# A transformer block moved to even/odd token pairs in the two row halves of TensorE, with DMA transposes, 121-query blocks, two-bank PSUM groups and a mixed phase order

## The chip, the cores and the metric

The kernel runs on one core of one Trainium2 chip. The metric is device time in microseconds (us) of one execution; "span" is the same thing inside one profiled execution, a few us shorter. TensorE is called PE, its weight loads PEld, VectorE DVE, ScalarE ACT, GpSimd POOL, and SP is the engine that issues the DMAs. PSUM is the memory that matmuls write; results are copied out of it by ACT or DVE. The granted clock is the share of its full clock that PE got. This is a one-core program, and a run counts as slow when it is more than 1.5% above the fastest of its kernel.

## The reference, cut to what matters

Two blocks in series on 2048 tokens of width 448, all bf16. The attention has 16 heads of 28, and each query sees 8 keys two tokens apart. So even tokens only attend to even ones and odd tokens to odd ones.

```python
h  = x + A(layernorm(x), wqkv, wo)            # attention: keys at t, t-2, ..., t-14
h2 = h + B(layernorm(h), w1, w2, w3, w4)
# B(y): g = gelu(layernorm(y) @ w1); shift g's four channel groups by -1, +1, -2, +2 tokens
#       x1 = y + shifted(g) @ w2;  x1 + gelu(layernorm(x1) @ w3) @ w4      (w3: 448 x 1792)
```

So a token passes three layernorms, and each is followed by a transpose (tokens to columns) and a projection.

## The kernel before

The kernel is written as a list of operations in *program order*. A planner on the host then fixes an order for each engine: it always takes the operation that can start earliest, and among those within 100 ns of each other the one written first. It knows durations from constants in the code. On the chip every engine works through its fixed order; semaphores hold it where data is missing. So the order in which phases are written matters in two ways: it breaks ties, and it decides who gets a shared buffer first, because a later-written user of a buffer waits for the earlier-written one.

The contraction of 448 is cut in four pieces of 112 rows. Layernorm output is transposed on PE, through PSUM, and copied out by ACT or DVE:

```python
    def transposes(ls, dst):
        for half in range(2):
            T = tile()
            for il in range(4):
                for cc in range(2):
                    c = 2 * half + cc
                    S.add("pe", "transpose", 64.0,
                          out=T(lambda p, o=cc * 512 + il * 128: p[0:KC, 0, :].bitcast(BF16)[:, o:o + 128]),
                          in_=lntm[:, ls, il, c * KC:(c + 1) * KC], identity=ident[:])
            copy(dst(half), T(...), 1024, 0.52)
    # QK: for each of 8 tiles: 4 matmuls, 112 rows, 128 weights columns, 512 tokens
    # W3: for each of 14 tiles: 4 matmuls, 112 rows, 512 tokens; gelu by ACT, 512 wide
```

The phases are written unmixed (cut):

```python
    phase_A1(0) ... phase_QK(0); phase_V(0); ... phase_att(0); phase_QK(1) ... phase_att(3)
    phase_WO(2); phase_WO(3)
    phase_B1(0); phase_B1(1); phase_B2(0); phase_B1(2); phase_B1(3)      # layernorm 2, W1; W2
    phase_W3(0); phase_B2(1); phase_W3(1); phase_B3(0); ...              # layernorm 3, W3; W4
```

## Time and profile before

252.07 us median of 3 runs. First the page of the profiled execution: busy time per engine, then PE's busy share and granted clock in 40 equal slices (a digit is tenths), then the engines' shares of the chain that ended last (work and waits followed back from the last instruction), then three groups of instructions (count, busy us, mean ns of one). All have one line number, L1100 here, because one line of the kernel issues every operation.

```profile
span 250.6 us, 4082 instructions
...
PE 224.6 (90%) x1681; PEld 112.9 (45%) x1681; DVE 138.2 (55%) x306; ACT 120.7 (48%) x175; POOL 46.2 (18%) x71
...
PE   0799799999979998898995999899998999899992
...
PEclk9999659999965995589998899999999999999998
...
PE 72%; DVE 16%; ACT 5%; POOL 2%; issue 2%; DVEq 0%
...
L1100 PE MATMUL ps<-actT,w_s 112*128 112x512 bf16 (+1 forms) x288 | 64.2, 382 | 1.2 <-DVE mv L1100 1.1
...
L1100 PE MATMUL ps<-ident,lntm 128*112 128x128 bf16 x192 | 18.8, 250 | 11.2 <-DVE lntm L1100 11.2
...
L1100 ACT ACTIVATE pt<-ps 110x1024 bf16<-110x1024 f32 x32 | 30.3, 1030 | 7.8 <-PE ps L1100 7.8
```

PE is the bound: it is busy 90% of the span and it is 72% of the chain. The clock row shows 5 and 6 in three places in the first half. They follow stretches like this one, from the timeline of PE (start us, duration, what, and what ended the idle time before it):

```profile
66.82 1.24 PE L1100 MATMUL ps<-qT,kT 28*110 28x103 bf16 x40
68.39 0.46 PE L1100 MATMUL ps<-qT,kT 28*110 28x103 bf16 x10 [0.33 <-ACT pt L1100]
69.30 0.46 PE L1100 MATMUL ps<-qT,kT 28*110 28x103 bf16 x10 [0.46 <-ACT pt L1100]
70.22 0.46 PE L1100 MATMUL ps<-qT,kT 28*110 28x103 bf16 x10 [0.46 <-ACT pt L1100]
```

PE works 0.46 us and waits 0.46 us, because each pair of heads needs one exponential of 1 us on ACT (the ACT line above).

For the comparison I break a span into terms. *Work*: every matmul at its full-clock pace in the traces (216 ns for 512 columns, 189 for 448, 56 for 128; where two or four matmuls run side by side, that divided by two or four). *Switches*: 96 ns for each change between full, half-row, quarter-row and quarter-column tiles, read from the gaps in the trace. *Half clock*: the work of the matmuls that started before the first clock record or in a half-clock record, counted once more. *First* and *tail*: before PE's first and after its last matmul. *Waits*: the rest. Work and half clock are estimates from these durations; the other terms are read directly.

| | span | work | switches | half clock | first | tail | waits |
|---|---|---|---|---|---|---|---|
| before | 250.6 | 193.1 | 5.5 | 18.1 | 7.0 | 4.8 | 22.2 |

### The profile page before, as it was taken

To read this page: it belongs to the slowest core of one execution; us is meant where nothing else is said; L and a number is where in the kernel's file an instruction comes from. 1 tells how busy PE (TensorE), PEld (TensorE's weight loads), DVE (VectorE), ACT (ScalarE), POOL (GpSimd) and SP (SyncE) were. 2 spreads that over 40 slices of the span, in tenths; PEclk is the share of its full clock that TensorE was granted. 3 is DMA by queue.
4 is the path that set the end of the run, shared out by engine and by line. 5 is a ranking of instruction groups with operands and counts; after the bars stand their busy time and mean duration, and the time that the engine had idled before them with its cause. 6 is when DMAs were issued, how large, how long until landed. Compare 5 with 4: busy or idle time off the path is not lost.

```text
span 250.6 us, 4082 instructions
## 1 busy us (share of the span) xinstructions
PE 224.6 (90%) x1681; PEld 112.9 (45%) x1681; DVE 138.2 (55%) x306; ACT 120.7 (48%) x175; POOL 46.2 (18%) x71
## 2 busy tenths in 40 slices
PE   0799799999979998898995999899998999899992
PEld 0336345645533556354544533533554345533550
DVE  7596862595785677877999602700385008700220
ACT  2468836896485649645422575166002740156000
POOL 8512200010031003003017200800016000710000
PEclk9999659999965995589998899999999999999998
DMA  6999900070610052007000000000100000000111
GB/s 164 291 222 232 275 12 5 8 171 5 146 29 0 8 131 44 3 7 173 0 1 3 0 0 0 21 18 0 36 15 25 0 16 23 20 18 0 42 39 42
DMA packets 11696, 14.07 MB, mean 56 GB/s; under 512 B 2136, under 2 KB 10712, under 8 KB 11160
## 3 DMA queue, kind: packets, MB, share of 16 engines
q1 hardware_dynamic: 11672, 13.75, 22.7%
q8 instruction: 15, 0.25, 0.4%
q14 instruction: 9, 0.07, 0.1%
HBM read 11.65 MB, written 1.97 MB: 54 GB/s over the span
## 4 chain that ended last, share of the span: by engine, by line
PE 72%; DVE 16%; ACT 5%; POOL 2%; issue 2%; DVEq 0%
PE ps L1100 72%; DVE st L1100 4%; DVE lntm L1100 4%; ACT pt L1100 3%; DVE xb L1100 2%; POOL rstd L1100 2%; DVE mv L1100 1%; DVE oT L1100 1%; ACT hT L1100 1%; ACT actT L1100 1%; DVE pt L1100 1%; ACT arena L1100 0%; POOL vtmp L1100 0%; DVE xin L1100 0%; DVE msk L1100 0%
## 5 line engine op out<-in xcount | busy, mean ns | idle before, releaser
L1100 PE MATMUL ps<-actT,w_s 112*128 112x512 bf16 (+1 forms) x288 | 64.2, 382 | 1.2 <-DVE mv L1100 1.1
L1100 ACT ACTIVATE arena<-ps 128x512 bf16<-128x512 f32 (+1 forms) x67 | 40.0, 597 | 28.0 <-PE ps L1100 27.8
L1100 PE MATMUL ps<-w_s,arena 128*128 128x448 bf16 x224 | 43.9, 353 | 0.0
L1100 PEld LDWEIGHTS ps<-actT,w_s 112*128 112x128 bf16 (+1 forms) x288 | 25.9, 106 | 37.8 <-ACT arena L1100 15.2
L1100 PE MATMUL ps<-hT,arena 112*128 112x512 bf16 x128 | 39.4, 453 | 0.5 <-ACT hT L1100 0.2
L1100 DVE TENSOR_TENSOR ost<-ps,xb 128x448 bf16<-128x448 f32 x16 | 10.0, 622 | 54.2 <-PE ps L1100 54.1
L1100 ACT ACTIVATE pt<-ps 110x1024 bf16<-110x1024 f32 x32 | 30.3, 1030 | 7.8 <-PE ps L1100 7.8
L1100 ACT ACTIVATE actT<-ps 112x1024 bf16<-112x1024 bf16 x10 | 10.0, 1028 | 44.2 <-PE ps L1100 44.2
L1100 POOL TENSOR_SCALAR vtmp<-mv 128x4 f32<-128x4 f32 (+1 forms) x19 | 4.6, 241 | 143.0 <-DVE mv L1100 142.3
L1100 PEld LDWEIGHTS ps<-w_s,arena 128*128 128x128 bf16 x224 | 21.5, 98 | 20.5 <-DVE xb L1100 0.6
L1100 PE MATMUL ps<-ident,lntm 128*112 128x128 bf16 x192 | 18.8, 250 | 11.2 <-DVE lntm L1100 11.2
L1100 PEld LDWEIGHTS ps<-ident,lntm 128*112 128x112 bf16 x192 | 15.9, 152 | 14.5 <-DVE lntm L1100 12.1
L1100 DVE TENSOR_TENSOR pt<-pt,msk 110x1024 bf16<-110x1024 bf16 x32 | 21.0, 684 | 1.7 <-ACT pt L1100 1.7
L1100 DVE BATCH_NORM_STATS2 st<-xin 128x6 f32<-128x448 bf16 x32 | 19.2, 601 | 2.4 <-DMA xin<-in_A_x_dram 1.9
L1100 PEld LDWEIGHTS ps<-hT,arena 112*128 112x128 bf16 x128 | 11.6, 108 | 17.9 <-issue 6.0
L1100 POOL TENSOR_TENSOR rstd<-vtmp,mhalf 128x4 f32<-128x4 f32 (+1 forms) x19 | 18.5, 972 | 1.6
L1100 POOL TENSOR_TENSOR xb<-xb,xin 128x448 bf16<-128x448 bf16 x16 | 16.7, 1072 | 1.5 <-DVE lntm L1100 1.5
L1100 DVE TENSOR_TENSOR xb<-ps,xb 128x448 bf16<-128x448 f32 x16 | 9.6, 600 | 13.4 <-PE ps L1100 13.1
L1100 PE MATMUL ps<-qT,kT 28*110 28x103 bf16 (+1 forms) x320 | 13.2, 229 | 3.8 <-ACT pt L1100 3.5
L1100 PE MATMUL ps<-wo_s,oT 128*128 128x448 bf16 x64 | 16.2, 403 | 0.4 <-DVE oT L1100 0.3
L1100 PE MATMUL ps<-arena,hT 112*110 112x448 bf16 x80 | 15.8, 353 | 0.0
L1100 ACT ACTIVATE gT<-ps 112x512 bf16<-112x512 f32 x16 | 9.6, 600 | 12.3 <-PE ps L1100 12.3
(52 smaller groups left out, 188.5 us busy)
## 6 DMA issues: line engine op xcount, KB each, us to landing
rzb<-rz_scratch SPq DMA_DIRECT2D x16, 256.0 KB, 4.4
w_s<-in_B_w_dram SPq DMA_DIRECT2D x2, 1568.0 KB, 18.0
out_dram<-ost SPq DMA_DIRECT2D x16, 112.0 KB, 1.7
xin<-in_A_x_dram SPq DMA_DIRECT2D x3, 448.0 KB, 8.9
arena<-in_A_wqkv_dram SPq DMA_DIRECT2D x3, 392.0 KB, 6.2
w_s<-in_B_w_dram SPq DMA_DIRECT2D x2, 392.0 KB, 10.5
xin<-in_A_x_dram SPq DMA_DIRECT2D x4, 112.0 KB, 2.2
wo_s<-in_A_wo_dram SPq DMA_DIRECT2D x4, 98.0 KB
```

The costliest lines, as they stand in the source:

```text
L1100: inst = getattr(eng, op.meth)(**op.kw)
```

## The change

Even and odd tokens go to separate banks of PSUM and to separate halves of the PE rows. 448 = 7 x 64: seven pairs of 64-row matmuls, each pair side by side, replace four 112-row matmuls per token. Layernorm output is transposed by DMA, straight into the row-half layout. Attention uses 121 queries against 128 keys, so that the weights are 128 columns and four row groups run at once. Results leave PSUM two banks at a time. The planner learns macros, tile modes and two-bank groups. Cut to its core:

```diff
+    def ln_to_HT(slot, kind, m, src):              # m: one of 8 blocks of 128 token pairs
+        sl = lctr[0] % NL                          # NL = 3 buffers of one block each
+        lctr[0] += 1
+        for a in range(2):
+            normalize(slot, kind, 2 * m + a, ln[:, sl, :, a, :], src[:, 2 * m + a, :]...)
+        S.add("sp", "dma_start_transpose", 1400.0, chan=ch("tr"), lat=128 * 896 * 2,
+              out=HT[:, :, 16 + 128 * m:16 + 128 * m + 128], in_=ln[:, sl, ...])
...
+    def phase_QK(u):
+        for c in range(4):
+            T = tile(2)
+            for w in range(2):
+                for b in range(KB):                # 7 pieces of 64
+                    for a in range(2):             # even tokens: rows 0-63; odd: rows 64-127
+                        ... mm(T(p[:, a, 256 * w:...]), wqk_p[half[a], b, ...], HT[half[a], b, 256 tokens])
+            copy(QK[...], T(p.rearrange("p a (w n) -> p a w n", w=2)), 1024)
...
+    def wload(chan, dst, src):                     # half-row weights are loaded twice
+        for u in range(2):
+            dma(chan + "ab"[u], dst[half[u]], src.rearrange("(b k) n -> k b n", k=64), ...)
...
+    setup()                                        # x0, x1, Q/K and V weights, x2..x7
+    for m in range(4):
+        phase_LN1(m)
+    weights()                                      # WO, W1, W2, W3, W4: 5.9 MB
+    unit_qkv(0); phase_att(0); unit_qkv(1); phase_LN1(4); phase_LN1(5); phase_att(1)
+    wo_ln2(0, 1, 2)
+    unit_qkv(2); phase_W1(0, 1); phase_W1(1, 2)
+    phase_LN1(6); phase_LN1(7); phase_att(2)
+    for m in (0, 1): phase_W2(m); phase_LN3(m)
+    phase_W3(0); unit_qkv(3); phase_W4(0); wo_ln2(3, 4); phase_att(3); phase_W1(3, 2)
+    ...
```

The change also *mixes* the MLP phases among the attention phases.

## The prediction

> **What bounds it now.** TensorE. Busy per engine: PE 224.6 of 250.6 us (90%), DVE 138, ACT 121. The chain that ended last is 72% PE. Start-to-start times from the trace, full clock: 512-column matmuls 216 ns, 448-column 189 ns, transposes 56 ns, the 28-row score matmuls 25 ns each (two at once), the 32-column value matmuls 13 ns (four at once). Times the counts: Q/K 128 x 216 = 27.6, V 80 x 189 = 15.1, transposes 192 x 56 = 10.8, W1 13.8, W3 48.4, W4 42.3, W2 and WO 12.1 each, scores 8.0, values 4.2: 194 us. The other 56 us: 7 us until the first transpose (10.4 until the first projection), some 5 us of tail, and about 40 us of waits and half clock. The clock records show 37 us at half clock in four stretches, three starting just after PE was paced by the exponentials (1 us each) in an attention stage, the fourth after the wait for the layernorm near 131-134 us. I put their cost at 18 us.
>
> **What the change does to PE.** 448 = 4 x 112 = 7 x 64: two 64-row matmuls, even and odd tokens, run side by side, so 7 half passes cost 3.5 instead of 4. If a pair of N columns takes what one full matmul takes (N/2.4 + 2.5 ns), I estimate Q/K 24.9, V 11.9, W1 12.5, W3 43.5. W4, W2, WO stay. Scores: four row groups at once and 288 instead of 320 matmuls, about 3.9; values 3.9. Transposes leave PE (-10.8). Sum 167 us: 27 us less. The 128-key block also brings the fast weight load, which the Trainium skill ("TensorE: Matmul & The Clock Gate", Weight-path perf modes) ties to 128 weights; the trace agrees in kind: 98 ns for a 128-column load, 130 ns for 110.
> Added: tile-mode switches, 96 ns each in the trace (56 now). I count about 100 after: +4 us.
>
> **Other engines.** The transposes' PSUM copies go (about 21 us of ACT and DVE); PSUM evictions get wider and fewer. 24 DMA transposes appear; no trace has one; I guess 4 us each until landed, hidden by other phases except at the start. Weights for half rows load twice (about 3 MB more), the Q/K ones before the first matmul: at the 290 GB/s seen early, the first projection starts near 13.5 us instead of 10.4. SP issues more, still far from full.
>
> **Critical path.** PE is the bound, so nearly all of the 27 us counts; start +3, switches +4. MLP phases are mixed among attention phases, so PE has fill work while exp runs; I expect waits and half clock to fall from 40 us to 15-20 but not vanish: the first two attention stages still have little fill work. 167 + 10 (switches) + 13.5 (start) + 4.5 (tail) + 15-18 = 210-213.
>
> **Predicted:** 211 us, 8 in 10 between 198 and 227. Faster by over 2%: 0.95; within 2%: 0.03; slower: 0.02.
>
> **Right or wrong, by the profile:** pairs of 64-row matmuls starting a few ns apart, a pair of 256 columns every 110 ns or so; PE's sum of start-to-start work near 167 us plus switches; half-clock time in the slices under 20 us, sitting before 80 us; no ident transposes; DMA transposes landing in 3-5 us; first matmul of Q/K at 12-15 us.
>
> **What would make it wrong:** pairs not overlapping (weight loads in series or a PSUM conflict: +40 us); DMA transposes landing in 8 us or more, starving W1 and W3; attention still pacing PE so the clock halves as before (+10 to 20); DVE, now reading two banks at a time, becoming the pacer in the early stages; or much better mixing, with no half clock after 30 us (below 200).

## The result

283.81 us median of 4 runs against 251.68 before. The ratio of the fast runs is 1.128 (95% interval 1.122 to 1.134): slower by 13%. Ratios here are the mean time of one kernel's fast runs over that of the other's of the same rounds, so not quite the ratio of the medians quoted.

The page after, with the lines that answer to those before:

```profile
span 280.3 us, 5851 instructions
...
PE 192.5 (69%) x2567; PEld 128.4 (46%) x2567; DVE 138.4 (49%) x296; ACT 102.0 (36%) x109; POOL 51.3 (18%) x92
...
PE   0009640699906540999999935569996489999892
...
PEclk9999955599986796699999977599999669999999
...
PE 59%; DMA 17%; DVE 11%; ACT 6%; issue 3%; POOL 2%; SPq 1%; DVEq 0%
...
L1259 PE MATMUL ps<-HT,w_s 64*128 64x256 bf16 (+1 forms) x1064 | 61.7, 279 | 19.2 <-DMA HT<-ln 10.8
```

And one line of the view of the DMAs (count, median us from issue to landing):

```profile
HT<-ln SPq DMA_TRANSPOSE x24, 2.9
```

PE is busy 32 us *less* and the span is 30 us *longer*. The half-row group shows that the core of the idea works: 1064 matmuls in 61.7 us are 58 ns each although one lasts 279, so pairs overlap. No identity transposes are left. But PE's row has zeros and fours in it, and DMA, which was not in the chain before, is 17% of it. The last line gives the transposes' median time to landing, 2.9 us, which is no worse than predicted.

| | span | work | switches | half clock | first | tail | waits |
|---|---|---|---|---|---|---|---|
| before | 250.6 | 193.1 | 5.5 | 18.1 | 7.0 | 4.8 | 22.2 |
| after | 280.3 | 165.2 | 5.9 | 19.4 | 21.6 | 4.9 | 63.3 |

The 28 us of work are gained, as predicted. 15 are lost at the start and 41 in waits. Who waits, from the waits view (us in total, times, longest):

```profile
PE ps L1259 <- DMA HT<-ln: 42.2, 3, 21.6
...
PE ps L1259 <- DVE pt L1259: 13.7, 6, 7.1
...
PE ps L1259 <- DVE QK L1259: 7.8, 2, 5.9
...
PE ps L1259 <- DVE xb L1259: 4.9, 1, 4.9
```

Three waits for a transposed layernorm make 42 us. One is the start, 21.6 us. The second is this (timeline, SP and PE):

```profile
24.72 27.08 SPq L1259 DMA_TRANSPOSE HT<-ln  x3
...
41.50 0.60 PE L1259 MATMUL ps<-pt,vt 128*32 128x121 bf16 x16 [1.41 <-DVE pt L1259]
...
51.84 1.68 PE L1259 MATMUL ps<-wv_s,HT 64*128 64x448 bf16 x8 [9.75 <-DMA HT<-ln]
```

Three transposes that SP normally issues in 1.22 us each took 27 us to issue, behind the weight loads issued just before. The third is this:

```profile
98.37 3.20 PE L1259 MATMUL ps<-wo_s,QK 128*128 128x448 bf16 x16 [1.86 <-DVE QK L1259]
...
105.28 1.24 SPq L1259 DMA_TRANSPOSE HT<-ln  x1
...
109.44 1.23 SPq L1259 DMA_TRANSPOSE HT<-ln  x1
...
111.33 1.22 SPq L1259 DMA_TRANSPOSE HT<-ln  x1
...
112.42 1.46 PE L1259 MATMUL ps<-HT,w_s 64*128 64x256 bf16 x12 [10.85 <-DMA HT<-ln]
```

Here nothing is slow. WO of two blocks ends at 101.6. For each block then come the residual, two statistics, the power, the normalization and the transpose of the second layernorm, one after the other; the two blocks share DVE with each other and with a product of attention. The second block's transpose is issued at 109.4, and PE has nothing to do for 10.9 us until W1 can start at 112.4.

### The profile page after: what moved, and what is told of

Read it like the earlier page. It is cut to its first block, busy times and chain, and to the rows that moved or that the text cites. A ratio compares the mean times of both kernels' runs of the same rounds, so it can differ in the third digit from the quotient of the medians.

```text
span 280.3 us, 5851 instructions
## 1 busy us (share of the span) xinstructions
PE 192.5 (69%) x2567; PEld 128.4 (46%) x2567; DVE 138.4 (49%) x296; ACT 102.0 (36%) x109; POOL 51.3 (18%) x92
## 4 chain that ended last, share of the span: by engine, by line
PE 59%; DMA 17%; DVE 11%; ACT 6%; issue 3%; POOL 2%; SPq 1%; DVEq 0%
PE ps L1259 59%; DMA HT<-ln 15%; DVE st L1259 3%; ACT pt L1259 3%; DVE xb L1259 2%; DMA h<-in_A_wqkv_dram 2%; DVE xin L1259 2%; DVE QK L1259 1%; ACT QK L1259 1%; POOL rstd L1259 1%; SPq L1259 1%; DVE mv L1259 1%; DVE ln L1259 1%; ACT osb L1259 1%; ACT L1259 0%
## 5 line engine op out<-in xcount | busy, mean ns | idle before, releaser
L1259 PE MATMUL ps<-HT,w_s 64*128 64x256 bf16 (+1 forms) x1064 | 61.7, 279 | 19.2 <-DMA HT<-ln 10.8
L1259 PEld LDWEIGHTS ps<-HT,w_s 64*128 64x128 bf16 x1064 | 55.2, 101 | 25.8 <-DMA HT<-ln 16.2
L1259 ACT ACTIVATE QK<-ps 128x1024 bf16<-128x1024 f32 (+2 forms) x24 | 22.7, 953 | 53.2 <-PE ps L1259 53.2
L1259 DVE TENSOR_TENSOR pt<-pt,msk 128x968 bf16<-128x968 bf16 (+1 forms) x34 | 22.0, 653 | 24.8 <-ACT pt L1259 24.8
L1259 ACT ACTIVATE pt<-ps 128x968 bf16<-128x968 f32 (+1 forms) x34 | 31.0, 976 | 6.5 <-PE ps L1259 6.5
L1259 PE MATMUL ps<-HT,arena 64*128 64x256 bf16 x448 | 26.3, 273 | 0.4 <-ACT QK L1259 0.4
L1259 POOL TENSOR_TENSOR rstd<-vtmp,mhalf 128x2 f32<-128x2 f32 (+1 forms) x34 | 24.1, 709 | 2.8
L1259 PEld LDWEIGHTS ps<-HT,arena 64*128 64x128 bf16 x448 | 21.9, 96 | 4.9 <-issue 0.9
L1259 PE MATMUL ps<-w_s,arena 128*128 128x448 bf16 x112 | 21.5, 353 | 1.1 <-ACT arena L1259 1.1
L1259 PE MATMUL ps<-w_s,h 128*128 128x448 bf16 x112 | 21.5, 353 | 0.5 <-ACT h L1259 0.5
L1259 PE MATMUL ps<-wo_s,QK 128*128 128x448 bf16 x64 | 14.6, 385 | 7.8 <-DVE QK L1259 7.8
```

The costliest lines, as they stand in the source:

```text
L1259: inst = getattr(eng, meth)(**kw)
```

## The experiments

All kernels gave the right result. Medians are of 4 runs each, all fast but one of act_q and two of s_ln1pe; the kernel before had medians of 250.3 to 251.7 in these rounds.

### First: is it the DMA queue?

My first theory was the visible one: the transposes stand in a queue behind 5.9 MB of weights. The rivals: DMA transposes are slow by themselves; the bandwidth is short whatever the queue; or the loss is not in the DMAs at all. In the first three runs the orders of PE, DVE and POOL were left exactly as in the changed kernel.

**late_sp** moves the weight loads back in SP's order:

```diff
+    move(("wo0", ..., "w1a", "w1b", "w2"), after="LN1_3")   # after transpose 4
+    move(("w3a", "w3b"), after="att_0")
+    move(("w4",), after="att_1")
```

> Only the order of DMA issues on SP is changed: WO, W1, W2 are issued after the fourth transpose (LN1 of pair block 3), W3 after the first attention block's scratch traffic, W4 after the second's. Every other engine keeps its order. Theory 1 (transposes wait in the same queue behind 5.9 MB of weights): the 9.7 us gap of PE at 42-52 us goes, transposes 3 and 4 land within about 5 us of being issued, span falls by 10 to 20 us (264-274). Theory 2 (DMA transposes are slow by themselves): they land as late as before, span within 2% of 284. The first matmul stays at about 20-22 us in both.

Measured: 285.64 us, equal to the changed kernel within 1%. The gap at 42 us went, transposes 3 and 4 landed 2.9 us after issue, and the longest landing, now that of the first transpose, fell from 27.1 to 10.8 us. But another wait took its place. From the timeline of late_sp, first SP, then DVE and PE:

```profile
46.30 12.07 SPq L1293 DMA_DIRECT2D rzb<-rz_scratch  x8
58.40 1.35 SPq L1293 DMA_DIRECT2D w_s<-in_B_w_dram  x2
```

```profile
76.89 0.35 DVE L1293 RECIPROCAL rzp<-zp 128x32 f32<-128x32 f32 x1 [11.99 <-DMA zp<-osb]
...
78.08 0.59 PE L1293 MATMUL ps<-QK 28*128 28x121 bf16 x16 [10.94 <-DVE osb L1293]
```

The small transfer of the next attention block's denominators (zp) now stood behind W3, and DVE waited 12 us for it. PE stood still for 10.9 us from 67.1 on. So theory 1 was right about the gap and the landings and wrong about what they are worth; theory 2's span came, but not its reason.

**act_q** issues the same loads from ACT, so from another queue:

```diff
+    for o in [o for o in sp if o.tag == "weights"]:
+        sp.remove(o); o.eng = "act"                         # placed after ACT's setup copies
```

> Same orders, but the eleven weight loads of WO and W1 to W4 are issued by ACT after its setup copies, so they stand in another DMA queue than the transposes. Theory 1a (order within one queue): transposes 3 and 4 land in under 8 us, the gap at 42-52 us shrinks below 4 us, span 264-276. Theory 1b (the 16 engines' bandwidth, whatever the queue): the transposes crawl along with the weights, gap stays over 6 us, span over 278.

Measured: 288.99 us (three fast runs of four, 287.71 to 289.23). The loads did stand in another queue (the DMA view has q10 beside q1), and the first of them were issued at 12.3 us instead of 14.6. The gap moved forward: the first matmul came at 24.9, and a wait of 6.3 us followed at 27.7. The transposes crawled as before (SP's timeline, then the times to landing from the view of the tile HT):

```profile
14.71 34.66 SPq L1290 DMA_TRANSPOSE HT<-ln  x4
```

```profile
DMA to landing us min/median/max: 2.9/3.0/29.8
```

So the bandwidth rival (1b) holds for the transposes: a second queue does not let them past the bulk. The Trainium skill ("DMA: Bandwidth & Descriptors", Issuing engines are not separate DMA queues) says that DMAs run on the same 16 engines and interleave whatever engine started them; this run agrees, 29.8 us against 27.1 in one queue.

**front** is late_sp with the first two transposes issued ahead of the V weights and of x2 to x7:

```diff
+    sp[:] = [x0, x1, wqk..., tr(LN1_0), tr(LN1_1)] + [wv..., x2 ... x7] + rest
```

> late_sp, and besides SP issues x0, x1, the Q/K weights, then transposes 1 and 2, and only then the V weights and the other six x blocks. Theory 1: first matmul near 13-15 us instead of 21.6, span 5 to 9 us below late_sp. If the start is bound by something else than the queue (layernorm, copies), first matmul stays over 18 us.

Measured: 285.75 us, first matmul at 20.5. This edit was badly made: PE's first operation is a V projection, and its weights were now issued only at 13.6, behind the transposes, which had to wait for the layernorm. The view of HT says so, "what its engine waited for":

```profile
  DMA wv_s<-in_A_wqkv_dram: 20.5, 1
```

So the span tests nothing. But the trace does: with the V weights and x2 to x7 behind them, the first two transposes landed 3.0 us after issue; in the changed kernel the first one took 11.4. So the late landing there comes from the bulk ahead of the transpose, not from the transpose itself.

**pe_tr** takes the DMA transposes away: seven 128x128 PE transposes into one bank and one copy per block. Here the planner makes new orders.

```diff
-        S.add("sp", "dma_start_transpose", ...)
+        T = tile()
+        pe([("transpose", dict(out=T(...), in_=ln[:, sl, b, :, :]..., identity=ident[:])) for b in range(KB)], ...)
+        S.add("flex", "tensor_copy", ...)           # out of PSUM, by ACT or DVE
```

> The row-half layout kept, but each of the 24 DMA transposes is made of seven 128x128 transposes on PE and one copy out of PSUM; the planner makes new orders. PE work +9 us, copies +15-20 us spread on ACT and DVE. If the DMA transposes (queueing or latency) cost the 57 us of waits: first matmul near 15 us, no gap over 5 us before 60 us, span 240-262. If the loss is in the row-half layout or in the mixing of phases: span stays over 270.

Measured: 274.61 us, so 9 less, with the first matmul at 10.2 us. Waits were still 55.5 us. The start gives 11 us and the waits 8, of which 9 go into PE's transposes and 2 into half clock. With no DMA transpose anywhere, most of the waits stayed. The DMA theory had fallen as the main cause.

### Second: is it the order of the phases?

The largest share of the waits that stayed, 19 us in pe_tr, was like the one at 101.6: PE waits for a normalized block, the end of a serial chain, with nothing else to run. My new theory 3 was the mixing.

**unmix** changes only the order in which the phases are written. It follows the old kernel's order of stages; every other part of the change stays, and so does the planner. Two things come with it: all eight first layernorms are written first, and W1 takes the blocks two by two, so PE has 2511 matmuls instead of 2567 for the same work.

```diff
-    ... phase_att(1); wo_ln2(0, 1, 2); unit_qkv(2); phase_W1(0, 1) ... phase_W3(0); unit_qkv(3) ...
+    for m in range(8): phase_LN1(m)
+    weights(); unit_qkv(0); phase_att(0); unit_qkv(1); phase_att(1); unit_qkv(2); WO(0..2) ... phase_att(4); WO(5..7)
+    for m in range(8): phase_LN2(m)
+    phase_W1(0, 2) ... phase_W1(6, 2)
+    for m in range(4): phase_W2(m); phase_LN3(m)
+    phase_W3(0) ... phase_W4(3)
```

> After late_sp and front, which took the DMA gap away and won nothing. Only the order in which the phases are written (and so planned) changes: first all projections and attention with the WO projections, then all second layernorms and W1, then W2, third layernorms, W3 and W4, as in the kernel before. All parts of the change stay: row halves, DMA transposes, the weights' place, PSUM groups. Theory 3 (mixing made PE wait on a serial chain per pair block: WO, layernorm, transpose, W1, W2, layernorm, transpose, W3): waits of PE fall from 63 to under 45 us, span 252-268. Rival (the waits come from DMA transposes or weights, whatever the order): span stays within 3% of 284.

Measured: 252.00 us, ratio to the kernel before 1.007 (0.999 to 1.015). The waits are about 40 us, as theory 3 said. Order alone is worth some 30 us (32 by the medians, 30 by the ratios). PE's row and clock:

```profile
span 249.9 us, 5752 instructions
...
PE   0005943079999957419639988999999999999992
...
PEclk9999975559999995956967999999999999999999
```

The second half is solid nines; the start and the wait for a transpose behind the weights at 42 us are still there, and the stretch from 90 to 140 us is thin.

**unmix_pe** and **unmix_late** add to unmix the PE transposes, or the W3 and W4 loads in three pieces after attention blocks 0, 1 and 2.

> unmix with PE transposes in place of the DMA transposes. If order and transposes cost separately: about 10 us under unmix, 240-255, first matmul near 10 us; if unmix alone already hides the transposes in the middle, only the start gains (about 10 us) less 9 us of PE work: equal to unmix within 2%.

> unmix, with W3 and W4 loaded in three pieces, each issued after the scratch traffic of attention blocks 0, 1 and 2, and planned so. If the weights' queueing still costs in the unmixed order (a PE gap near 42-52 us there), it goes: 4 to 10 us under unmix. If not, equal within 2%.

Measured: 254.07 and 249.40 us. In this order PE transposes win nothing (the start falls to 10.2 us, 9 us of PE work come back), so the DMA transposes in the middle are hidden here: after 52 us no wait of PE in unmix ends on one. The weights' place is worth about 1%, "equal" by the text above: the gap at 42 us went, but three waits of 6 to 7 us for a transpose came later.

**ln1_early_pe** stays with the mixed order and pe_tr, but writes the first layernorms of blocks 6 and 7 before attention block 1.

> The mixed order and PE transposes (pe_tr), but the first layernorms of pair blocks 6 and 7 are written before attention block 1, so they do not queue for one of the three layernorm buffers behind the second layernorms of blocks 0 to 2. If the three small buffers and their order starve the fourth projection block: 8 to 15 us under pe_tr's 274.6 (260-267). If not: within 2% of it.

Measured: 269.38 us, 5 less than pe_tr. That is 1.9%, so by the text above it counts as no effect, and it comes from another round. This run does not show that the buffers matter; the fourth part does.

### Third: is mixing itself bad?

I then let the kernel's own planner search over legal phase orders, with its DMA constants set to the times measured here and the W3 and W4 loads in pieces. Three results were run: with the first layernorm's transposes on PE and the others by DMA (s_ln1pe), all by DMA (s_dma), all on PE (s_pe). The search moved phases at random, kept what shortened the plan, and kept all data dependences.

> The row-half layout with a phase order found by a search over orders with the kernel's own planner: first layernorms early and transposed on PE, second and third by DMA, W3 and W4 loaded in pieces after attention blocks 0 and 1; MLP phases are still mixed among attention phases (W1, W2, W3 of pair blocks 0 and 1 before attention block 2). If mixing as such is what cost, this order must be no better than unmix_late (249). If it was the order given together with three layernorm buffers and late transposes: first matmul near 10 us, waits of PE under 30 us, span 225-242, faster than the kernel before by 4 to 10%.

> A searched order with all transposes by DMA (weights in pieces as in s_ln1pe). First matmul stays near 21 us; otherwise waits as low as in s_ln1pe: 8 to 12 us slower than it, 235-250.

> A searched order with all transposes on PE. First matmul near 10 us, PE work 9 us above s_dma, DVE and ACT with 24 copies more: 230-246, within 3% of s_ln1pe if DMA latency in the middle is hidden there.

| | median us | ratio to before (95%) |
|---|---|---|
| s_ln1pe | 230.37 | 0.910 (0.901 to 0.919), two of four runs fast |
| s_dma | 236.57 | 0.942 (0.936 to 0.949) |
| s_pe | 231.35 | 0.923 (0.917 to 0.929) |

All beat both kernels. The kernel before was not searched over, so this does not tell what the new layout is worth when each has its best order. The page of s_pe:

```profile
span 228.5 us, 6081 instructions
...
PE   0159998998896491887999999999999999999990
...
PEclk9999999999999766599999999999999999999999
```

And the order of s_ln1pe is itself mixed: W1, W2 and W3 of blocks 0 and 1 are written before attention block 2. So theory 3 as I had put it is wrong as well. Mixing is not the cause; *this* mixed order is. s_dma's range was met. By fast runs it is 8 us slower than s_ln1pe (whose two fast runs took 227.2 and 229.7), less than the 11 us by which its first matmul is later (21.6 against 10.2).

### Fourth: what in the given order?

Four rungs from the changed kernel, each the one before it with a single edit, except that lad1 makes two at once.

```diff
 lad1: changed order; W3 and W4 in pieces; planner's DMA times as measured
 lad2: - DMA transposes of the first layernorm      + the same on PE
 lad3: - phase_LN1(6), phase_LN1(7) after wo_ln2(0, 1, 2)      + before phase_att(1)
 lad4: - phase_W3(0), phase_W4(0) before phase_att(3)      + just before phase_W3(1)
```

> Rung 1, from the changed kernel: its phase order, W3 and W4 in pieces after attention blocks 0 and 1, and the planner's DMA times set to those measured here (a transpose 2.9 us, other transfers 1.7 us plus bytes at 220 GB/s). If the planner's wrong DMA times and the weights' place made most of the loss: span under 260. If not: 264-276.

> Rung 2: lad1 with the eight transposes of the first layernorm on PE. The start gains about 11 us for 3 us of PE work: 8 to 16 us under lad1.

> Rung 3: lad2 with the first layernorms of pair blocks 6 and 7 written before attention block 1 instead of after the second layernorms of blocks 0 to 2. If they had to queue for the three layernorm buffers: 8 to 14 us under lad2, and the long wait of PE for the transposes of the second layernorm (some 10 us near 75-100 us) shrinks below 5 us because the fourth projection block can fill it. If the buffers do not matter: equal within 2%.

> Rung 4: lad3 with W3 and W4 of pair blocks 0 and 1 written after attention block 4 instead of before attention block 3. If early MLP work used up what later has to cover the layernorm waits of the last blocks: 4 to 8 us under lad3, with the waits moved out of the stretch after 140 us. If not: equal within 2%.

| | median us | step | work | half clock | first | waits |
|---|---|---|---|---|---|---|
| after | 283.81 | | 165.2 | 19.4 | 21.6 | 63.3 |
| lad1 | 280.37 | -3 | 165.2 | 24.6 | 21.7 | 56.8 |
| lad2 | 271.57 | -9 | 168.4 | 23.6 | 10.2 | 54.2 |
| lad3 | 256.48 | -15 | 168.4 | 15.2 | 10.2 | 48.2 |
| lad4 | 252.43 | -4 | 168.4 | 19.4 | 10.2 | 41.3 |
| s_ln1pe (profile of a slow run) | 230.37 | -22 | 168.4 | 11.2 | 10.2 | 26.8 |

lad1 ended 4 us above its range, lad3 gained 1 us more than its range, lad2 and lad4 are inside. lad4's 4 us are also within the 2% that its text calls equal; PE's waits of over 2 us after 140 us fell from 15 to 7 us there. Together the rungs give back 31 of the 32 us. The largest single edit moves two first layernorms. The reason is in `sl = lctr[0] % NL`: there are three layernorm buffers, handed out in program order. In the given order the first layernorm of block 7 takes the buffer after the second layernorm of block 1, so it can only be written when that one, at the end of a chain of attention, WO and statistics, has been transposed. The fourth projection block, which needs nothing but x, stands behind it, and so PE has nothing to fill the wait with.

**lad2_nl4** tests just that: lad2 with a fourth buffer, no phase moved.

```diff
-    NL = 3
+    NL = 4
```

> lad2 with four layernorm buffers instead of three, no phase moved. lad3 gained 15 us by moving the first layernorms of blocks 6 and 7 ahead of the second layernorms of 0 to 2. If that was the queue for the buffers: lad2_nl4 gains 6 to 14 us over lad2's 271.6 (258-266), and the 9 us wait of PE near 86 us shrinks. If it was only the planner giving earlier-written phases precedence on DVE: within 2% of lad2.

Measured: 262.62 us, 9 of the 15. PE at the same place, first lad2, then lad2_nl4 (timelines of PE):

```profile
83.60 2.28 PE L1304 MATMUL ps<-wo_s,QK 128*128 128x448 bf16 x6
94.89 2.52 PE L1304 MATMUL ps<-HT,w_s 64*128 64x256 bf16 x21 [9.01 <-DMA HT<-ln]
```

```profile
83.76 2.43 PE L1304 MATMUL ps<-wo_s,QK 128*128 128x448 bf16 x12
86.12 1.70 PE L1304 MATMUL ps<-HT,arena 64*128 64x256 bf16 x28
87.66 2.93 PE L1304 MATMUL ps<-wv_s,HT 64*128 64x448 bf16 x28
90.52 0.40 PE L1304 MATMUL ps<-QK 28*128 28x121 bf16 x16
...
95.81 0.60 PE L1304 MATMUL ps<-pt,vt 128*32 128x121 bf16 x16 [3.81 <-DVE pt L1304]
```

With three buffers PE goes from WO into a 9 us wait for W1's input. With four, projections (HT,arena and wv_s,HT) and attention stand in that place, and the wait that is left is 3.8 us. They are the fourth block's: by 90 us all 448 Q/K matmuls have run, while lad2 still has 336 when its wait ends at 94.9. Over the whole profile, waits and half clock together fall by 7 us; later waits for a transposed block have grown (up to 9.6 us). A fifth buffer does not fit: with five the changed kernel does not build, since it runs out of SBUF, the on-chip memory, where the half-row weights take more room than before (W3 alone 7 x 1792 columns instead of 4 x 1792).

The 22 us between lad4 and s_ln1pe (24 by fast runs) I did not take apart. They are the rest of the order. In the terms, two thirds are PE's waits (41.3 to 26.8) and one third is the half clock that comes with them (19.4 to 11.2); which phase moves make it stays open.

## Why the prediction was wrong, point by point

- **"Sum 167 us: 27 us less."** Right: 165.2 after and 193.1 before. Pairs of 64-row matmuls do overlap. No step of the result comes from slow matmuls.
- **"+4 us" for tile-mode switches, "I count about 100".** There are 61 of them, 5.9 us; harmless.
- **"The first projection starts near 13.5 us."** Mis-sized: 21.6 us. The weights were counted, but x2 to x7 and the V weights go ahead of the first transpose as well, and the transpose is a DMA that has to get through: 11.4 us to landing behind them, 3.0 us in the run front, where they come after it. lad2 gives back 9 us by taking PE for these eight transposes.
- **"24 DMA transposes ... 4 us each until landed, hidden by other phases except at the start."** The size was right in the median (2.9 us), wrong for those that met the bulk of the weights (up to 27.1 us). I had listed 8 us as a danger, but thought of it as the transpose's own slowness. Taking these transposes out of the queue won nothing by itself (late_sp), since another small transfer then stood behind the same bytes, and since the chain had other waits to show; a second queue did not free them at all (act_q).
- **"MLP phases are mixed among attention phases, so PE has fill work while exp runs; I expect waits and half clock to fall from 40 us to 15-20."** This is the step that failed. Waits and half clock went from 40.3 to 82.7 us. I read the mixed order as parallel work by its intent, and did not ask of each wait which operation could fill it. unmix shows the order to be worth some 30 us with nearly all else equal; lad3 and lad2_nl4 show one mechanism in it: work that was free to run was chained, by three buffers handed out in written order, behind work that was not. The order that s_ln1pe uses is mixed too and has 38 us of the two terms, so the intent was sound and the order was not.
- **"Half-clock time ... under 20 us, sitting before 80 us."** The size was right, 19.4 us; the place was wrong: the clock after has low stretches from 35, 83, 93, 107, 165, 175 and 219 us, each during or just after waits of PE. No run here changes the one without the other, so I count them as a consequence.
- **"DVE ... becoming the pacer in the early stages"**, listed as a danger, was not tested by itself. DVE was busy 138 us in both kernels. But it does hold PE up in places: from 78.5 to 85.6 us PE waits for a product of attention (pt, 7.1 us), while DVE is busy for 6.9 of these 7.1 us, mostly with second layernorms. PE's waits that end on DVE are 16 us before, 7 of them the start, and 27 after. How much of the loss this is no run separates.

## What to carry to other kernels

A change that shortens the bound engine's work pays only if the waits do not grow, so cost a new phase order like a new instruction: for every wait of the bound engine, name the operation that fills it, and follow that operation's inputs *and its buffers* back. Buffers handed out in program order chain independent work together; when a layout costs memory and leaves fewer or smaller buffers, look there first. Where the orders are planned, search the order again after a rebuild: nearly the same instructions ran in 284, 252 and, with DMA constants as measured and the weights in pieces, 237 us.

## What the Trainium skill lacked or had wrong

- "TensorEngine Tiling (Array Packing)", Key Properties, says that changing the tiling mode drains TensorE, but gives no cost. The gaps in these traces are 91 to 100 ns per change, between any two of full, 64-row, 32-row and 32-column tiles, where nothing else was waited for.
- "TensorE: Matmul & The Clock Gate", Back-to-back issue gap, gives about 131 ns per matmul for a sustained stream with N = 512. The 224 W3 matmuls of the kernel before started 216 ns apart, which is what that section's isolated formula says.
- The same page, "What's actually happening", has the clock return after at least one busy window of about 3.4 us. In the kernel before three of the four half-clock stretches inside PE's work lasted 10.2 us or more; during one of them (26.5 to 36.8 us) the timeline shows PE working from 27.7 on without a pause, 9.1 us, full-array matmuls alternating with 28-row and 32-column ones. Whether such work counts as busy in the page's sense no run here shows.
- "DMA: Bandwidth & Descriptors", DMA Transpose (X-bar), has no duration for a transpose from SBUF to SBUF; other places of the skill give bandwidths and sequencer cycles, but no time to landing. For 128 x 896 bf16 the traces show 1.22 us of issue on SP and 2.9 us to landing on idle DMA engines, up to 23 us of issue for a single one and up to 29.8 us to landing behind bulk loads, during which SP issues nothing else.
